# Seven products for eight from the third batch on in a kernel of attention and a two-layer product, with the second weight prepared during the first two batches

## The chip, the cores and the metric

The kernel runs on one core of one Trainium2 chip. A time is the device time in microseconds (us) of one execution, and of several executions the median is given. A profiled execution also has a span, from the first to the last instruction that the profiler recorded, which is a little shorter than its device time. The engines are named as the profile names them: PE (TensorE) multiplies, with PEld for its weight loads; DVE (VectorE) and ACT (ScalarE) work on tiles; POOL (GpSimd) works on tiles and starts the loads; SP (SyncE) starts the transposing copies and the stores.

## The reference

Eight sequences ("batches") of 384 tokens pass through an attention with 16 query heads and 4 key/value heads of 64 columns, and the result through two matrix products with a squared relu between them.

```python
q: (8, 16, 384, 64)   k, v: (8, 4, 384, 64)
w_in: (1024, 2048)    w_out: (2048, 1024)

scores = np.matmul(q, k.transpose(0, 1, 3, 2)) / np.sqrt(64)
attn = softmax(scores)
x = np.matmul(attn, v).transpose(0, 2, 1, 3).reshape(8 * 384, 16 * 64)
h = np.maximum(x @ w_in, 0.0)
return (h * h @ w_out).astype(np.float32)
```

## The kernel before

**Stages.** Each batch b has an up product (384 rows of x by w_in, "up-b") and a down product (384 rows of the squares by w_out, "down-b"), one after the other. Between their matmuls lie the attention pieces of the next batches: the scores q·k (L437; their exponentials go to `expT`, L447), the probabilities by the values (L463 on all 128 rows of the array, L504 on two concurrent halves of 64 rows), the division by the row sums (L472 and L478), and the largest magnitude of each piece of x (L1438).

**Order.** The program is not written in the order in which it runs. A class `Recorder` takes every instruction group with what it reads and writes and an assumed cost, and keeps a clock for each engine. A loop picks TensorE's next piece among the candidates by these clocks, and between the pieces `upkeep` hands out work to the other engines from queues, each entry with a condition: `d_q` (sums for the down product), `w_q` (parts of w_in), `w2_q` (parts of w_out), `lazy` and `m_q` (ranges of x). Then each engine gets its list in that order, with semaphore waits where the readers and writers demand them. An engine works its list strictly in order.

**Seven products for eight.** From batch `SB` = 2 on, the up product splits both factors into two by two blocks and makes seven block products where the plain way makes eight (`strassen`, L884), with sums of blocks of x (L642) and of w_in (L724, L729; w_in itself is scaled in place by L738, with one subtraction, L742). The block products are evicted from the accumulator banks by L855, L860, L863 and L868, and then squared (L770, L778, L782). From batch `FAST` = 3 on, the down product does the same with pairs of row tiles (`pair_of`). A batch has three row tiles of 128. Pair "A" joins tiles 0 and 1 of batch b. Every second batch also makes pair "D" of the tile 2 of the batch before and its own. The copy L1157 keeps that earlier tile. `sum_ops` makes the sums of a pair (L1138, part of them on GpSimd), `done` the evictions (L1054 to L1062) and one addition on GpSimd (L1091). Since batches 3 to 7 are five, tile 2 of batch 7 is left without a partner. It is multiplied the plain way (`downs`, `down_part`, L1249), after L1162 has restored a block of w_out.

The matmuls of seven products run as two concurrent streams on the halves of the array (L924 for the down product). The plain down products of batches 0 and 1, and the plain tile of batch 7, use all 128 rows (L1249). The plain down product of batch 2 goes through the stream too. The up product of batch 0 uses whole rows (L563), that of batch 1 halves (L600, `quad`, evicted by L613, squared by L618). Plain results are evicted by `store` (L1274, L1281).

**Preparation of w_out.** The block sums are kept in f16, so w_out is first scaled to a common range. `fold2` takes sixteen sums of squares (L1174, on ScalarE), `roots2` turns them into bounds by two shifts (L1180, L1181), `top_of` takes the largest (L657) and spreads it (L659), `top_spread` sends it through TensorE (L669) and back (L673), and `o_units` makes the factor (L1186, L1188). Then `scaled2` writes scaled blocks into `area` (L1191), `less2` subtracts them from each other (L1199), `here2` scales w_out in place (L1191) once nothing plain reads it any more, and `apart2` makes the last difference (L1206). In the kernel before, the conditions of `w2_q` place the folds between 101.2 and 120 us, the maximum at the end of down-1, the blocks from there to 167.7 us, their differences in down-2, the scaling in place between 173.2 and 190 us, and the last difference behind it in up-3.

**Space.** `expT` of a batch has two halves, the second of them in `area`, where the blocks of w_out and two of the eight `hr` tiles live later too. `LEAN` = 3 is the first batch that has only the first half, so that at most half of its scores can be made before its values are multiplied. `LATE` = 4 is the first batch whose values are loaded straight to their place.

The two conditions that place the maximum and the scaled blocks of w_out:

```python
w2_q.append((lambda: not spread_q and not w_q, [], roots2, "vector"))
def cleared():
    return "o_beta" in R.writer and x_done[LEAN - 1] == NKC and up_over()
```

## Time and profile before

| | us |
|---|---|
| three runs | 404.82, 405.20, 405.56 |
| median | 405.2 |
| profiled execution, its device time | 404.96 |
| its span | 403.1 |

Stages by the first and last matmul of each, in us of the span:

| batch | up | down | what of w_out is prepared there |
|---|---|---|---|
| 0 | 15.8 to 52.1 | 52.1 to 73.1 | |
| 1 | 73.2 to 103.3 | 103.3 to 126 | folds, maximum, first block |
| 2 | 126 to 151 | 151 to 176 | blocks, differences, first of the scaling in place |
| 3 | 176 to 203.4 | 203.4 to 219.5 (A) | rest of the scaling in place, last difference |
| 4 | 219.5 to 244 | 244 to 272 (A, D) | |
| 5 | 272 to 297.5 | 297.5 to 311.1 (A) | |
| 6 | 311.1 to 336.3 | 336.3 to 361 (A, D) | |
| 7 | 361 to 380.5 | 380.5 to 403.1 (A, one plain tile) | |

How to read the profile's lines: a row of a timeline begins with the start, then the length, the engine, the line of the kernel and the operation, then what it writes and reads, with partitions by elements. A row of the waits gives the waiting engine and line, the engine and line that ended the wait, and the total, the number and the mean. A row of the stages gives a stretch, its length, and the busy time of each engine with the number of its instructions.

### The profile page before, as it was taken

Reading aid. Unit: us, or ns where it says so; the run is one execution under the profiler, and the core shown is the slowest. Engines: PE = TensorE matmul, PEld = TensorE weight load, DVE = VectorE, ACT = ScalarE, POOL = GpSimd, SP = SyncE. Lnnn points to the kernel's source line nnn. Section 1 sums busy time; section 2 is a strip of 40 time slices with the busy share of each in tenths; the row PEclk is TensorE's granted clock in tenths of the full one; section 3 lists DMA queues with packets and bytes.
Section 4 is the critical chain, followed back from the end, with each engine's and each line's share of the span. In section 5 each row is a group of like instructions: output and inputs, shape, how many; then the busy total and the mean of one; then the engine's idle time right before and its main releaser. Section 6 shows DMA issues by size and latency. Waiting matters only on the chain. (4 is left out here: it accounts for less than half of the span.)

```text
span 403.1 us, 15107 instructions
## 1 busy us (share of the span) xinstructions
PE 392.0 (97%) x6784; PEld 292.4 (73%) x6784; DVE 313.2 (78%) x646; ACT 261.5 (65%) x365; POOL 145.5 (36%) x167
## 2 busy tenths in 40 slices
PE   8999999999998999998998999999999999999997
PEld 5665754456546998788874998749996998649944
DVE  3699879924967879998989797867878888936655
ACT  7949940087985998897884677735985686115610
POOL 8675600168230230044563444223532152114500
PEclk9999999999999999999999999999999999999999
DMA  9999999993993172699677632598160311212003
GB/s 173 191 197 185 208 187 186 146 246 56 156 147 123 32 93 42 137 157 113 78 105 121 115 43 57 114 179 161 23 101 29 101 33 33 80 52 81 4 28 130
DMA packets 97200, 44.75 MB, mean 111 GB/s; under 512 B 77552, under 2 KB 91120, under 8 KB 97136
## 3 DMA queue, kind: packets, MB, share of 16 engines
q0 software_dynamic: 36672, 17.44, 34.7%
q1 hardware_dynamic: 59792, 25.86, 30.8%
q8 instruction: 53, 0.87, 0.9%
q10 hardware_dynamic: 672, 0.49, 0.4%
q14 instruction: 11, 0.09, 0.1%
HBM read 35.65 MB, written 12.58 MB: 120 GB/s over the span
## 5 line engine op out<-in xcount | busy, mean ns | idle before, releaser
L447 ACT ACTIVATE expT<-ps 128x1024 bf16<-128x1024 f32 (+1 forms) x118 | 115.3, 1012 | 19.7 <-PE ps L437 19.2
L884 PE MATMUL ps<-xT,w_in_sb 64*128 64x192 f16 x1152 | 85.5, 243 | 0.9 <-DVE y_sb L1062 0.6
L924 PE MATMUL ps<-w_out_sb,h2T 64*128 64x512 f16 (+1 forms) x464 | 84.9, 376 | 0.0
L884 PEld LDWEIGHTS ps<-xT,w_in_sb 64*128 64x128 f16 x1152 | 70.7, 94 | 4.9 <-DVE y_sb L1062 1.0
L782 POOL TENSOR_TENSOR h2T<-hr 128x384 f16<-128x384 f32 (+1 forms) x49 | 40.5, 843 | 49.0 <-ACT hr L770 48.6
L437 PE MATMUL ps<-qT,kT 64*128 64x256 bf16 (+2 forms) x336 | 52.1, 324 | 0.5 <-DVE qT L408 0.2
L884 PE MATMUL ps<-s_all,wx 64*128 64x192 f16 x768 | 52.2, 242 | 0.0
L1249 PE MATMUL ps<-w_out_sb,h2T 128*128 128x512 bf16 (+3 forms) x240 | 49.4, 365 | 0.0
L868 DVE TENSOR_TENSOR hr<-ps,hr 128x384 f32<-128x384 f32 x72 | 39.7, 555 | 10.3 <-PE ps L884 6.9
L924 PEld LDWEIGHTS ps<-w_out_sb,h2T 64*128 64x128 f16 (+1 forms) x464 | 38.9, 94 | 11.0 <-DVE hr L855 0.4
L924 PE MATMUL ps<-area,xT 64*128 64x512 f16 x224 | 43.6, 376 | 1.0 <-DVE y_sb L1056 1.0
L884 PEld LDWEIGHTS ps<-s_all,wx 64*128 64x128 f16 x768 | 44.0, 94 | 0.8
L600 PE MATMUL ps<-xT,w_in_sb 64*128 64x384 bf16 x448 | 42.7, 323 | 0.5 <-DMA xT<-area 0.3
L770 ACT ACTIVATE hr<-hr,bits 128x384 f32<-128x384 f32 x59 | 35.0, 608 | 10.1 <-DVE hr L868 9.8
L1249 PEld LDWEIGHTS ps<-w_out_sb,h2T 128*128 128x128 bf16 (+1 forms) x240 | 22.4, 98 | 24.9 <-issue 0.6
L504 PE MATMUL ps<-v_aug,expT 64*128 64x65 bf16 x1440 | 38.2, 190 | 1.6 <-issue 1.3
L504 PEld LDWEIGHTS ps<-v_aug,expT 64*128 64x128 bf16 x1440 | 35.2, 94 | 3.2 <-issue 1.7
L884 PE MATMUL ps<-xT,wx 64*128 64x192 f16 x384 | 33.2, 243 | 0.0
L860 ACT COPY hr<-ps 128x384 f32<-128x384 f32 x29 | 13.8, 477 | 29.9 <-PE ps L884 29.0
L884 PE MATMUL ps<-s_all,w_in_sb 64*128 64x192 f16 x384 | 33.0, 242 | 0.0
L600 PEld LDWEIGHTS ps<-xT,w_in_sb 64*128 64x128 bf16 x448 | 21.4, 94 | 15.9 <-DMA xT<-area 0.6
L863 DVE COPY hr<-ps 128x384 f32<-128x384 f32 x43 | 23.7, 555 | 8.1 <-PE ps L884 6.1
(147 smaller groups left out, 744.7 us busy)
## 6 DMA issues: line engine op xcount, KB each, us to landing
out_dram<-y_sb SPq DMA_DIRECT2D x44, 256.0 KB, 2.4
w_in_sb<-in_moe_w_in_dram POOLq DMA_DIRECT2D x8, 512.0 KB, 14.6
w_out_sb<-in_moe_w_out_dram POOLq DMA_DIRECT2D x4, 1024.0 KB, 28.4
q_st<-in_q_dram POOLq DMA_DIRECT2D x19, 192.0 KB, 4.7
q_st<-in_q_dram POOLq DMA_DIRECT2D x4, 384.0 KB, 23.6
k_st<-in_k_dram POOLq DMA_DIRECT2D x6, 192.0 KB, 5.1
wx<-in_q_dram POOLq DMA_DIRECT2D x2, 384.0 KB, 7.7
out_dram<-area SPq DMA_DIRECT2D x3, 256.0 KB, 4.6
```

What stands on the lines that cost most here:

```text
L437: mm = pe.matmul(ps[:, base + x, m * wide:(m + 1) * wide], kT[at(b)][64 * x:64 * x + 64, u, :], q_cols(b, u // NJ, x, c0, c0 + wide))
L447: R.add("scalar", lambda e: e.activation(dst, src, AF.Exp, scale=0.125), reads=keys, writes=[("expT", slot(b, u), t) for u, _, _ in pieces ...
L504: m = pe.matmul(ps[:, p[x], n * DP:n * DP + D + 1], w, v_aug[b % 2][r, g * NJ + j, 0:D + 1], start=(n + j + y == 0), stop=(n + j + y == 2 ...
L600: m = pe.matmul(bank(4 + xs[x])[:, 0:S], w_in_sb[r, kc, c * 128:(c + 1) * 128], xT[b % NXT][r, kc, :], start=(phase < 2 and kc == 0), stop ...
L770: R.add("scalar", lambda e, val=val, to=to: e.activation(val, val, AF.Relu, scale=to), reads=[("hr", r)] + by, writes=[("hr", r)], cost=0. ...
L782: n = R.add(eng, lambda e, dst=dst, two=two: e.tensor_tensor(dst, two, two, ALU.mult), reads=[("hr", r)], writes=keys, cost=0.77 if other ...
L860: R.add("scalar", lambda e: e.copy(hr[r][:, :], src), reads=[("bank", at)], writes=[("hr", r)], cost=0.45, after=hr_read.pop(r, ()))
L863: R.add("vector", lambda e: e.tensor_copy(hr[r][:, :], src), reads=[("bank", at)], writes=[("hr", r)], cost=0.48, after=hr_read.pop(r, ()))
L868: R.add("vector", lambda e: e.tensor_tensor(hr[r][:, :], src, hr[r][:, :], ALU.add), reads=[("bank", at), ("hr", r)], writes=[("hr", r)], ...
L884: return lambda pe: pe.matmul(bank(at)[:, f * h:f * h + h], w[r, kc, c:c + 128], m[r, kc, :], start=(prod in (1, 5, 2) and y + f + kc == 0 ...
L924: return lambda pe: pe.matmul(bank(p.at)[:, 0:512], p.a(k, r), p.w(k, r), start=start, stop=stop, skip_group_check=True)
L1249: m = pe.matmul(bank(i)[:, 0:n], h2[:, c, i3 * 128:(i3 + 1) * 128], w2[:, c, c0:c1], start=(c == 0), stop=(c == NFC - 1))
```

## The change

Three of the constants that place things are lowered by one: `FAST` 3 to 2, `LEAN` 3 to 2, `LATE` 4 to 3. Batches 2 to 7 make their down products by pairs, which leaves no tile without a partner, so the plain tile of batch 7 and L1162's restoring of w_out are gone. With an even number of batches the D pairs fall to batches 3, 5 and 7.

- In the last batch the D pair ends in the order 7, 4, 3, and its last product is made on whole rows in two pieces of 384 and 128 columns (`whole_product`, new). `added`, `put` and `send` take a range of columns for it, and the second piece's store has a semaphore of its own.
- The folds of w_out go to a place of their own (`o_top`, in `s_all`), and may start once the folds of w_in are done, which is during down-0. The maximum may follow while w_in's parts are still waiting, in up-1. The blocks may be written as soon as batch 1's x is complete.
- `less2` and `apart2` may go to VectorE or GpSimd, whichever clock is free; GpSimd's assumed cost is 2.3 us.
- Half of w_in's scaling in place may begin in the last tiles of up-1, and on ScalarE.
- Score bursts of batches 2 and 3 may be placed inside down-1 (`loose`).
- Batch 1's and later evictions rotate over six `hr` tiles instead of eight. The largest magnitudes of x are taken for batch 2 too.

```diff
-    SB, LEAN, LATE, FAST = 2, 3, 4, 3
-    TINY, DOWN = 2.0 ** -100, 2.0 ** -12
+    SB, LEAN, LATE, FAST = 2, 2, 3, 2
+    TINY, DOWN, TAIL = 2.0 ** -100, 2.0 ** -12, 384
...
+    o_top = s_all.ap().rearrange("p a n c -> p (a n c)")[:, 2048:2080].bitcast(f32)
...
-                r = hr_n[0] % NHR
+                r = hr_n[0] % (NHR - 2 * (b > 0))
...
-                    r = hr_n[0] % NHR
+                    r = hr_n[0] % (NHR - 2 * (b > 0))
...
-              reads=["w_u1"], writes=[("w_16", q)], cost=3.6 if eng == "scalar" else 1.2, after=free)
+              reads=["w_u1"], writes=[("w_16", q)], cost=3.6 if eng == "scalar" else 1.75, after=free)
...
-        first, second, rest, carry = stream(products(b))
+        prods = products(b)
+        final = prods.pop() if b == B - 1 else None
+        first, second, rest, carry = stream(prods)
...
-            rest += [zipped([], carry[0] + carry[1])] + downs(b)
+            rest += [zipped([], carry[0] + carry[1][:1]), zipped([], carry[1][1:])] + whole_product(final)
...
+    def whole_product(p):
+
+        def part(c0, c1, at, fresh):
+            def mm(pe):
+                for k in range(p.n):
+                    m = pe.matmul(bank(at)[:, c0:c1], p.a(k, slice(0, 128)), p.w(k, slice(0, 128))[:, c0:c1], start=fresh and k == 0, stop=k == p.n - 1,
+                                  skip_group_check=True)
+                return m
+
+            def piece():
+                R.add("tensor", mm, reads=need, writes=[("bank", at)], cost=p.n * ((c1 - c0) / 2400 + 0.004))
+                p.done(at, c0, c1)
+
+            need = [r for k in range(p.n) for r in p.need(k)]
+            return NKC, need, [at], piece
+
+        return [part(0, TAIL, p.at, False), part(TAIL, 512, order[0], True)]
+
...
-            out += [first(4, b1)] + [second(*x) for x in ((1, b2), (2, b3), (5, b1), (6, b2), (7, b3), (3, b1), (4, bz))]
+            ends = ((7, b3), (3, b1), (4, bz)) if b < B - 1 else ((7, b3), (4, bz), (3, b1))
+            out += [first(4, b1)] + [second(*x) for x in ((1, b2), (2, b3), (5, b1), (6, b2)) + ends]
...
-        out[-1].done = lambda at: (tail_open.discard(b), last(at))
+        out[-1].done = lambda *at: (tail_open.discard(b), last(*at))
...
-        def added(at, g, a, to):
+        def added(at, g, a, to, c0=0, c1=512, after=()):
...
-            R.add("vector", lambda e: e.scalar_tensor_tensor(y_sb[z], bank(at), gs[g], y_sb[y], ALU.mult, ALU.add),
-                  reads=[("bank", at), ("g", g), ("y", y)], writes=[("y", z)], cost=0.68)
-
-        def put(who, x, name):
+            R.add("vector", lambda e: e.scalar_tensor_tensor(y_sb[z][:, c0:c1], bank(at)[:, c0:c1], gs[g], y_sb[y][:, c0:c1], ALU.mult, ALU.add),
+                  reads=[("bank", at), ("g", g), ("y", y)], writes=[("y", z)], cost=0.68 if c1 - c0 > 128 else 0.27, after=after)
+
+        def put(who, x, name, c0=0, c1=512):
...
-            send(bb, i3, 512 * x, 512 * x + 512, ys[name])
-
-        def done(prod, at):
+            send(bb, i3, 512 * x + c0, 512 * x + c1, ys[name], c0)
+
+        def done(prod, at, *cols):
...
+                ys["bank"] = at
...
+                if b == B - 1 and pair == "D":
+                    added(ys["bank"], g1, "b2", "b2", TAIL, 512, (R.writer[("y", ys["p5"])],))
...
-                added(at, g1, "b2", "b2")
-                put(one, 1, "b2")
+                added(at, g1, "b2", "b2", *cols)
+                put(one, 1, "b2", *cols)
...
-            return Product(at, a, w, lambda k: na(k) + nw(k), lambda at: done(prod, at), prod not in (3, 6))
+            return Product(at, a, w, lambda k: na(k) + nw(k), lambda *at: done(prod, *at), prod not in (3, 6))
...
-        R.add("scalar", lambda e: e.activation(junk, w2_piece(q, z, w_out_sb), AF.Square, accum_out=w_top[:, n:n + 1]),
-              reads=[("w_out",) + QS[q], "junk2"], writes=[("w_top", n), "junk2", ("hr", 6), ("hr", 7)], cost=1.15)
+        R.add("scalar", lambda e: e.activation(junk, w2_piece(q, z, w_out_sb), AF.Square, accum_out=o_top[:, n:n + 1]),
+              reads=[("w_out",) + QS[q], "junk2"], writes=[("o_top", n), "junk2", ("hr", 6), ("hr", 7)], cost=1.15)
...
-        t = w_top.bitcast(mybir.dt.int32)
-        keys = [("w_top", n) for n in range(16)]
+        t = o_top.bitcast(mybir.dt.int32)
+        keys = [("o_top", n) for n in range(16)] + [("S", 2)]
...
-        top_of(w_top, *keys)
+        top_of(o_top, *keys)
...
-    def less2(n, m, z):
+    def less2(n, m, z, eng="vector"):
...
-        R.add("vector", lambda e: e.tensor_tensor(a, a, c, ALU.subtract),
-              reads=[("T2", n, z), ("T2", m, z)], writes=[("T2", n, z)], cost=0.62)
+        R.add(eng, lambda e: e.tensor_tensor(a, a, c, ALU.subtract),
+              reads=[("T2", n, z), ("T2", m, z)], writes=[("T2", n, z)], cost=0.62 if eng == "vector" else 2.3)
...
-    def apart2(z):
-        R.add("vector", lambda e: e.tensor_tensor(w2_piece(3, z), w2_piece(3, z), w2_piece(2, z), ALU.subtract),
-              reads=[("w2", 3, z), ("w2", 2, z)], writes=[("w2t", z)], cost=0.6)
+    def apart2(z, eng="vector"):
+        R.add(eng, lambda e: e.tensor_tensor(w2_piece(3, z), w2_piece(3, z), w2_piece(2, z), ALU.subtract),
+              reads=[("w2", 3, z), ("w2", 2, z)], writes=[("w2t", z)], cost=0.66 if eng == "vector" else 2.3)
...
-            for i3 in range(0 if b < SB else 2, NJ):
-                last = b == B - 1 and (jj, i3) == (1, NJ - 1)
-                for c0, c1 in ((512, 896), (896, 1024)) if last else ((512 * jj, 512 * jj + 512),):
+            for i3 in range(NJ if b < SB else 0):
+                for c0, c1 in ((512 * jj, 512 * jj + 512),):
...
+                flags.add(("plain", b, NJ * jj + i3))
...
-    def send(b, i3, c0, c1, yb):
-        ysl = y_sb[yb][:, 0:c1 - c0]
+    def send(b, i3, c0, c1, yb, y0=0):
+        ysl = y_sb[yb][:, y0:y0 + c1 - c0]
...
-                            reads=[("y", yb)], writes=[("out", b, i3, c0)], dma=f"y{yb}", cost=0.6)
+                            reads=[("y", yb)], writes=[("out", b, i3, c0)], dma=f"y{yb}" + "z" * (y0 > 0), cost=0.6)
...
-                                                  spread_q.append((b % 2, lambda: (v_unit(b), measured.add(b))))), lambda: b != LEAN or pairs >= 8 * b))
+                                                  spread_q.append((b % 2, lambda: (v_unit(b), measured.add(b))))), lambda: b != 3 or pairs >= 8 * b))
...
+    def in_place(qq):
+        act, dve = [max(R.clock[x], R.clock["tensor"]) for x in ("scalar", "vector")]
+        w_in_place(qq, "scalar" if qq < 3 and act + 3.6 <= dve + 1.75 + 0.0 else "vector")
+
+    def columns_over():
+        return up_over() or ff["b"] == 1 and len(ff["tiles"]) <= 4
+
...
-        w_q.append((up_over, [], lambda qq=qq: w_in_place(qq, "vector")))
+        w_q.append((columns_over if qq < 2 else up_over, [], lambda qq=qq: in_place(qq)))
...
-        return "o_beta" in R.writer and x_done[LEAN - 1] == NKC and up_over()
-
-    w2_q = [(lambda: "w_u0" in R.writer and (ff["b"] > 1 or ff["b"] == 1 and below()), [("w_out",) + QS[n // 4]], lambda n=n: fold2(n), "scalar") for n in range(16)]
-    w2_q.append((lambda: not spread_q and not w_q, [], roots2, "vector"))
+        return "o_beta" in R.writer and x_done[LEAN - 1] == NKC
+
+    w2_q = [(lambda: not any(len(x) > 3 for x in w_q), [("w_out",) + QS[n // 4]], lambda n=n: fold2(n), "scalar") for n in range(16)]
+    w2_q.append((lambda: "w_u0" in R.writer and not spread_q, [], roots2, "vector"))
...
-            w2_q.append((cleared, [], (lambda *eng, n=n, qq=qq, z=z: scaled2(n, qq, z, *eng)) if m is None else (lambda n=n, m=m, z=z: less2(n, m, z)), "any" if m is None else "vector"))
+            w2_q.append((cleared, [], (lambda *eng, n=n, qq=qq, z=z: scaled2(n, qq, z, *eng)) if m is None else (lambda *eng, n=n, m=m, z=z: less2(n, m, z, *eng)), "any" if m is None else "either"))
...
-        w2_q.append((lambda: True, [], lambda z=z: apart2(z), "vector"))
+        w2_q.append((lambda: True, [], lambda *eng, z=z: apart2(z, *eng), "either"))
...
-                load_v(n)
+                if n < LATE:
+                    load_v(n)
...
-            lead = {"scalar": 0.1, "vector": 0.5 if ff["b"] == FAST else -9 if m_q or lazy else 1.0 if below() else 0.1}
-            able = [x for x in ("vector", "scalar") if eng in (x, "any") and R.clock[x] <= now + lead[x]]
+            lead = {"scalar": 0.1, "vector": -9 if m_q or lazy else 0.6 if below() else 0.4}
+            lead["gpsimd"] = 0.0
+            able = [x for x in {"any": ("vector", "scalar"), "either": ("vector", "gpsimd")}.get(eng, (eng,)) if R.clock[x] <= now + lead[x]]
...
-            w2_q.pop(0)[2](*(able[:1] if eng == "any" else ()))
+            w2_q.pop(0)[2](*(able[:1] if eng in ("any", "either") else ()))
...
+            loose = SB <= b <= SB + 1 and not split and ff["b"] == SB - 1 and len(ff["tiles"]) < 4
...
-            if b and not split and not beside:
+            if loose and b > SB:
+                ok = ok and (R.clock["scalar"] <= now + -99 or not (w2_q and w2_q[0][0]()))
+            if b and not split and not beside and not loose:
...
-                if b and not split and not beside:
+                if b and not split and not beside and not loose:
...
-                cand.append((t, 4 if beside else 0, "sc"))
+                cand.append((t, 4 if beside or loose and b > SB else 0, "sc"))
...
-        if split and at_edge and len(ff["tiles"]) < 4 and not (sc_q and sc_q[0][1]):
+        if split and at_edge and len(ff["tiles"]) < 4 and (not (sc_q and sc_q[0][1]) or ff["b"] == SB - 1):
...
+            widest_of(b, c - 3) if b >= FAST else None
...
+            if b >= FAST:
+                wide_q.append((b, c))
+                if c == 7:
+                    m_q.append((b, lambda b=b: widest_of(b)))
...
-            if b and not split and not beside:
+            if b and not split and not beside and not loose:
...

```

## The prediction

> **What bounds the kernel now.** I read the page's first two parts, then the waits of TensorE over the whole span, then the busy times by stage, and only then single instructions. "Up-b" and "down-b" are the up and the down product of batch b (0 to 7).
>
> ```profile
> span 403.1 us, 15107 instructions
> PE 392.0 (97%) x6784; PEld 292.4 (73%) x6784; DVE 313.2 (78%) x646; ACT 261.5 (65%) x365; POOL 145.5 (36%) x167
> ...
> PE ps L669 <- DVE top_w L659: 2.2, 2, 1.1
> PE ps L504 <- issue: 1.3, 1, 1.3
> PE ps L924 <- DVE y_sb L1056: 1.0, 1, 1.0
> ...
> PE ps L884 <- DVE y_sb L1062: 0.6, 2, 0.3
> ```
>
> TensorE is the bound: it is busy for 392.0 of 403.1 us, and its waits are few and can be listed one by one. So fewer matmul columns shorten the span one for one, and every other engine counts only where it makes TensorE wait. The stages show where that happens now:
>
> ```profile
> core 0: us, PE busy (x) PEld busy (x) DVE busy (x) ACT busy (x) POOL busy (x), PEclk, DMA share, GB/s
> 52.10:73.10 21.00, 21.00 (x104) 9.32 (x100) 16.93 (x32) 2.79 (x5) 1.69 (x1) 1.00 1.18 169
> ...
> 103.30:126.00 22.70, 21.57 (x107) 9.41 (x104) 17.91 (x34) 16.81 (x31) 5.17 (x5) 1.00 0.94 155
> ...
> 176.00:203.40 27.40, 25.74 (x740) 23.93 (x736) 24.67 (x54) 22.82 (x35) 14.64 (x16) 1.00 0.87 117
> 203.40:219.50 16.10, 14.04 (x146) 8.73 (x142) 14.74 (x27) 11.30 (x14) 7.27 (x8) 1.00 0.78 103
> 219.50:244.00 24.50, 24.01 (x668) 22.60 (x670) 20.37 (x49) 15.39 (x24) 11.67 (x14) 1.00 0.41 77
> ```
>
> The first column is the stretch, then its length, then the busy time of each engine. Down-0 (first row) is full. Down-1 (second) lacks 1.13 us of TensorE work: that is the wait for the maximum of w_out (L669 behind L659). Up-3, down-3 and up-4 (the last three) lack 1.66, 2.06 and 0.49 us, together 4.2 us. In up-3 the last parts of w_out are still being made, down-3 is the first stage with pairs, and VectorE is busy for 24.67 of 27.40 and 14.74 of 16.10 us in these two. In batch 5, where nothing is prepared, the same stages lack nothing. The granted clock is 1.00 throughout.
>
> **The change, part by part.** (1) *Fewer matmuls.* A plain down product takes 96 matmuls of 128 rows by 512 columns for three row tiles; a pair by seven products takes 56 where the plain way takes 64. Before, batches 3 to 7 make 7 pairs and one plain tile (7 x 56 + 32 = 424), and batch 2 is plain (96): 520. After, batches 2 to 7 make 9 pairs and nothing plain: 504. Two concurrent halves of such a matmul start 0.216 us after the two before them (five steps from 214.97 to 216.05 in TensorE's timeline of down-3). 16 x 0.216 = **-3.5 us**. The count is in the changed kernel's instruction order, so that the change does not do what it says is excluded.
>
> (2) *Switches between whole rows and halves.* L437 (scores) works on 64-row halves, L1249 and L463 on all 128 rows. Before, the scores of batch 2 all lie in up-1, whose L600 also works on halves. With LEAN = 2 only half of expT may be filled ahead, so nine of its eighteen score bursts, and five of batch 3, move into down-1, between L1249 and L463. Changes between 128 and 64 rows in TensorE's order rise from 48 to 70. The price of one:
>
> ```profile
> 16.18 0.39 PE L437 MATMUL ps<-qT,kT 64*128 64x512 bf16 x2
> 16.50 0.51 PE L538 MATMUL ps<-ident,o_sb 128*128 128x128 bf16 x6
> ...
> 181.19 0.38 PE L437 MATMUL ps<-qT,kT 64*128 64x512 bf16 x2
> 181.41 0.82 PE L884 MATMUL ps<-s_all,wx 64*128 64x192 f16 x16
> ```
>
> The first number of a row is its start. The same burst takes 0.32 us to the next start before 128-row work and 0.22 us before halves: 0.10 us for leaving, and entering costs as much (16.18 lies 0.42 us after the start of two L563 at 15.76, which need 2 x 0.16). 22 x 0.10 = **+2.2 us**; bounds 1.5 and 3.
>
> (3) *Start of up-1.* The maximum of w_out is now finished there: two shifts, L657 and L659 stand on VectorE ahead of the first L613, and L669 stands on TensorE between the pieces of the first quad. VectorE is late here already (the last L729 ends at 78.2 us and the second quad waits until 79.2 for banks 4 and 5). The four take 0.16 + 0.18 + 0.17 + 0.23 = 0.74 us; with the hand-over to TensorE **+0.9 us**; bounds 0 and 1.5 (the three L673, L1186, L1188 behind it also late). The sixteen squares of w_out move under down-0, where ScalarE works 2.79 of 21.0 us: 16 x 1.06 = 17 us fit, so they cost nothing; without that cover up-1's exponentials would start late.
>
> (4) *Down-1, the crowded stage.* By the changed order VectorE does there: 8 L472 and L478 (0.19 + 0.56, 6.0), two L738 (2.7), L742 (2.3), three L1199 (2.0), six L1274 (4.1), eight L1438 (4.3), four L642 (2.2), two L1191 (1.0) and eight small ones (1.7): 26.3 us. TensorE has 20.9 (the 96 matmuls of down-0) + 4.5 (144 L463 at 98.8 to 103.3, half of them just ahead of the stage) + 14 bursts x 0.22 + 2.2 of switches = 30.7 us. That leaves 4.4 us of slack, if nothing blocks VectorE. But GpSimd now makes 8 of the 12 L1199 subtractions, 6 of them here, and three of the four L1206 later. No row has one on GpSimd; the nearest has half the elements:
>
> ```profile
> L1138 POOL TENSOR_TENSOR xT<-h2T 128x512 f16<-128x512 f16 x5 | 5.8, 1159 | 11.7 <-PE ps L884 11.7
> ...
> 207.18 2.14 DVE L1138 TENSOR_TENSOR xT<-xT,h2T 128x512 f16<-128x512 f16 x1
> ...
> 207.12 1.90 POOL L1157 COPY area<-h2T 128x2048 f16<-128x2048 f16 x1
> ```
>
> So one costs 2 x 1.16 = 2.3 us, 13.9 for six. The last two rows show VectorE and GpSimd excluding each other: an L1138 that usually takes 0.42 us took 2.14 because a copy on GpSimd had started 0.06 us before, and the 1.0 us wait on L1056 above is what followed from it. L738, L742, L1199, L642 and L1191 (10.2 us) are of the kind that can be caught so; L478, L1274 and L1438 read PSUM or one tensor and run beside GpSimd. In the changed order L738, L1199, L738 and L742 stand against four subtractions in a row on GpSimd. If each waits 2.3 us less one 0.69 us copy that fits beside it, VectorE needs 26.3 + 4 x 1.6 = 32.7 us, 2.0 over TensorE; behind them are queued the evictions and the L1274 copies that free banks 6 and 7, and L1249 waits for those. With 0.3 us for the first burst, which waits for two evictions, **+2.3 us**. Bounds: 0 (VectorE first each time) and 9.5 (all six whole).
>
> (5) The wait for L659 near the end of down-1 goes: **-1.1 us**; another L669 takes its place for batch 2's range, inside the count of (4).
>
> (6) *Batches 2 to 4.* The 4.2 us of up-3, down-3 and up-4 go from there, since w_out is ready earlier and the first pairs lie in down-2. Part returns one batch earlier: eight scalings by L1191 (0.48 us on VectorE) and some of the L1206 lie in up-2, and down-2 has the same sums and copy on GpSimd as down-3 had. But its copy of the first product stands on ScalarE in the changed order, not behind the blocked sum, and L659 comes before the last three products, not after them. The 1.3 us without a releaser have no known cause and are left to chance. I take 1.2 us as returning: **-3.0 us**; bounds -4.2 and +1.
>
> (7) The last stage: one more pair in place of a plain tile, its last product in two pieces (384 and 128 columns) as the last plain one was. The 128-column eviction (0.35 us) may stand behind the 384-column one by 0.2 us: counted as nothing, bounds -0.5 and +0.5.
>
> Sum: 403.1 - 3.5 + 2.2 + 0.9 + 2.3 - 1.1 - 3.0 = 400.9 us of span. The profiled execution took 404.96 us, 1.86 more than its span, and the median of the three runs (405.2) lies 0.24 above it: **403.0 us**.
>
> **The rivals.** *The exclusion decides* (slower). All six blocks in down-1 cost 1.6 us: 26.3 + 9.6 - 30.7 + 0.3 = 5.5 in place of 2.3, and the three L1206 on GpSimd give up half of (6): +3.2 + 1.5, so 405.6 of span and 407.7 us. It decides from 8 us of blocks in down-1 on (6.4 are in the forecast): with 1.5 us of (6) gone, that passes 406.0 us. For it: the 2.14 us row and 10.2 us of catchable work. Against: of the ten VectorE instructions that this trace shows stretched by over 0.1 us beside GpSimd, TensorE waited behind four at most. The Trainium skill, page "SBUF — State Buffer", section "Who interferes with whom", says that a VectorE instruction with two SBUF inputs, or in a two-port mode, and a GpSimd instruction exclude each other for the whole of the one that came first. The 2.14 us row agrees; by that rule this rival is the likelier the more subtractions begin just ahead of VectorE's.
>
> *The stalls only move*: (6) is nought because up-2 and down-2 lose what up-3 and down-3 lost. 403.9 of span, 406.0 us. For it: the same rows of work on the same engines. Against: the order of L659 and of the first copy.
>
> *Everything fits*: (4) is nought and all 4.2 us of (6) are kept: 400.9 - 2.3 - 1.2 = 397.4, so 399.5 us. For it: 4.4 us of slack; against: the lateness of VectorE at the start of up-1.
>
> **How the numbers follow.** About 0.2% (0.8 us) is what a measurement of this kernel can tell from no change: faster is below 404.4, slower above 406.0. The forecast has 0.50 (its own range 400.8 to 405.2; 0.42 of it faster, 0.06 same, 0.02 slower), the exclusion 0.20 (0.19 slower, 0.01 same), moved stalls 0.17 (0.02 faster, 0.08 same, 0.07 slower), everything fits 0.13 (faster). Faster 0.57, same 0.15, slower 0.28. The range, 399.3 to 407.6, leaves out the half of the exclusion's chance above it and the better end of the last rival.
>
> **What would show it.** (1) 992 matmuls of the stream on halves, 16 at a new line, 192 of the plain kind. (2) Gaps of 0.1 us around each L437 in down-1. (3) L669 waiting some 0.9 us near 79 us. (4) In down-1, two-input VectorE instructions of 2 us beside L1199 on GpSimd, and L1249 waiting on L1274. (5) and (6) the stages of batch 3 without idle TensorE. I am wrong if down-1 loses over 5 us beside its switches, or if batches 2 and 3 together lose more than batches 3 and 4 did.

## The result, and the profile after

The changed kernel takes 418.0 us, median of four runs (416.9 to 418.3), against 405.4 us in the same series: ratio 1.0303, 95% interval 1.0272 to 1.0334. It is slower, and beyond the range. Every series of runs has its own runs of the kernel before (medians 405.0 to 405.5 us), and each ratio is to those; the changed kernel was timed in the first series alone, so differences to its 418.0 us reach across series. Two executions far above the others of their kernel, 573.2 us in subs_and_slot and 809.5 us in and_squares, are left out of the ratios and of what follows. The first parts of its page, and its waits of TensorE over the whole span (total, number, longest):

```profile
span 415.1 us, 15143 instructions
...
PE 393.8 (95%) x6764; PEld 286.8 (69%) x6770; DVE 333.2 (80%) x658; ACT 271.1 (65%) x372; POOL 174.8 (42%) x182
...
PE   8999999995999998998999999899999999999995
...
PEclk9999999999899999999999999999999999999999
```

```profile
PE ps L670 <- DVE top_w L660: 3.8, 3, 3.2
PE ps L885 <- issue: 1.8, 2, 1.0
PE ps L927 <- DVE y_sb L1084: 1.6, 3, 0.6
PE ps L601 <- DVE hr L614: 1.4, 1, 1.4
PE ps L927 <- DVE xT L1163: 1.4, 1, 1.4
```

The span is 12.0 us longer. TensorE is busy for about as long as before (393.8 us for 392.0), but idle for 21 us where it was idle for 11. The tenth slice, 93 to 104 us, is half empty, and the clock, full throughout before, dips just behind it. One wait of 3.2 us stands out. The line numbers of the changed kernel are higher: L660, L670 and L674 are the old L659, L669 and L673; L614, L619 and L625 the eviction and the squares of up-1; L739 the scaling of w_in (old L738); L1452 the range of a batch's values; L1163, L1182 and L1116 the sum, the copy and the addition of the pairs; L1216, L1224 and L1231 the scaling and the two subtractions.

The stages of up-1 to up-3, and down-4 (stretch, its length, busy time of PE, PEld, DVE, ACT, POOL, granted clock):

```profile
73.70:107.30 33.60, 27.80 (x359) 16.93 (x360) 32.98 (x57) 15.49 (x18) 18.85 (x18) 0.95 0.84 142
107.30:136.60 29.30, 28.77 (x202) 12.16 (x205) 24.49 (x39) 24.30 (x24) 17.50 (x11) 1.00 0.70 114
136.60:165.10 28.50, 26.36 (x704) 24.01 (x702) 26.31 (x59) 22.87 (x32) 16.50 (x16) 1.00 0.52 69
165.10:180.60 15.50, 15.24 (x215) 8.36 (x211) 14.88 (x29) 11.66 (x14) 8.26 (x7) 1.00 0.56 96
180.60:209.70 29.10, 26.42 (x768) 25.25 (x767) 23.86 (x51) 19.26 (x30) 16.02 (x18) 1.00 0.87 114
...
261.60:276.70 15.10, 13.60 (x138) 8.22 (x134) 12.97 (x27) 11.68 (x15) 4.88 (x6) 1.00 0.67 82
```

Batch 1 (the first two rows) takes 62.9 us where it took 52.9: this is 10.0 of the 12.0 us. Up-1 has 5.8 us of idle TensorE (before 0.5) and a clock of 0.95, though nine score bursts have left it. From up-2 to the last matmul the kernel needs 274.1 us, before 274.5: TensorE is busy for 3.9 us less there, but idle for 3.4 us more. The span ends 4.4 us behind the start of the last matmul, before 2.6, and 0.6 us is lost ahead of batch 1.

What happens in up-1 is read from three timelines, of VectorE, GpSimd and TensorE (start, length):

```profile
89.24 4.25 DVE L739 TENSOR_SCALAR w_in_sb<-w_in_sb,bits 128x4096 f16<-128x4096 bf16 x2
...
95.27 4.74 DVE L625 TENSOR_TENSOR h2T<-hr 128x384 bf16<-128x384 f32 x1
...
100.40 1.00 DVE L1452 TENSOR_REDUCE bits<-v_aug 128x1 f32<-128x384 bf16 x2
101.43 0.15 DVE L658 TENSOR_REDUCE bits<-bits 128x1 f32<-128x2 f32 x1
101.62 0.74 DVE L660 CAST top_w<-bits 128x128 bf16<-128x128 f32 x1
```

```profile
93.82 2.14 POOL L1224 TENSOR_TENSOR area<-area 128x1024 f16<-128x1024 f16 x1
95.91 1.61 POOL L619 TENSOR_TENSOR h2T<-hr 128x384 bf16<-128x384 f32 x2
97.47 2.11 POOL L1224 TENSOR_TENSOR area<-area 128x1024 f16<-128x1024 f16 x1
```

```profile
94.47 3.42 PE L601 MATMUL ps<-xT,w_in_sb 64*128 64x384 bf16 x40 [1.41 <-DVE hr L614]
...
97.73 1.46 PE L601 MATMUL ps<-xT,w_in_sb 64*128 64x384 bf16 x16
...
102.42 0.20 PE L670 MATMUL ps<-ident,top_w 64*128 64x64 bf16 x2 [3.22 <-DVE top_w L660]
```

A square on VectorE that takes 0.55 us elsewhere takes 4.74. It starts while a subtraction runs on GpSimd, and GpSimd goes on without a gap to two squares and a second subtraction. VectorE comes through only when that row of four is over, at 99.58. Behind the square stand the range of batch 3's values and its spreading (L1452, L658, L660), and L670, in order on TensorE, waits for it. An earlier wait, of 1.41 us, follows two scalings of w_in (L739) that take 4.25 us where one takes 1.28 alone. Behind the long wait the clock falls, as the same stretch shows, cut where the clock changes (column before the last two):

```profile
100.31:103.72 3.41, 1.30 (x27) 0.86 (x27) 3.34 (x8) 0.25 (x1) 0.82 (x1) 1.00 0.02 5
103.72:107.14 3.42, 3.28 (x62) 3.12 (x60) 3.32 (x10) 3.42 (x5) 2.60 (x4) 0.50 0.00 0
107.14:110.55 3.41, 3.36 (x18) 1.16 (x16) 2.94 (x6) 2.03 (x2) 3.41 (x2) 1.00 0.30 58
```

TensorE works at half speed for 3.4 us. That makes it busy for some 1.7 us longer, an estimate from half of 3.4 us; how much of it the kernel loses in the end is a question for the runs.

### The profile page after: what moved, and what is told of

Its sections match the earlier page's. It is cut to its first block, busy times and chain, and to the rows that moved or that the text cites. A ratio compares the mean times of both kernels' runs of the same rounds, so it can differ in the third digit from the quotient of the medians.

```text
span 415.1 us, 15143 instructions
## 1 busy us (share of the span) xinstructions
PE 393.8 (95%) x6764; PEld 286.8 (69%) x6770; DVE 333.2 (80%) x658; ACT 271.1 (65%) x372; POOL 174.8 (42%) x182
## 4 chain that ended last, share of the span: by engine, by line
PE 65%; DVE 16%; issue 8%; POOL 5%; DMA 3%; ACT 2%; POOLq 0%; DVEq 0%
PE ps L885 25%; PE ps L927 18%; PE ps L438 6%; PE ps L1273 5%; PE ps L505 4%; PE ps L601 4%; POOL area L1224 2%; DVE y_sb L1084 2%; PE ps L464 2%; DMA xT<-o_sb 2%; DVE hr L614 2%; DVE h2T L625 2%; DVE xT L1163 2%; DMA q_st<-in_q_dram 1%; PE ps L564 1%
## 5 line engine op out<-in xcount | busy, mean ns | idle before, releaser
L448 ACT ACTIVATE expT<-ps 128x1024 bf16<-128x1024 f32 (+1 forms) x127 | 124.7, 1015 | 28.5 <-PE ps L438 28.3
L927 PE MATMUL ps<-w_out_sb,h2T 64*128 64x512 f16 x336 | 73.3, 376 | 1.0 <-DVE y_sb L1084 0.6
L783 POOL TENSOR_TENSOR h2T<-hr 128x384 f16<-128x384 f32 x53 | 42.8, 826 | 58.3 <-ACT hr L771 58.1
L927 PE MATMUL ps<-area,xT 64*128 64x512 f16 x288 | 56.0, 376 | 1.4 <-DVE xT L1163 1.4
L1273 PE MATMUL ps<-w_out_sb,h2T 128*128 128x512 bf16 x186 | 43.2, 380 | 0.3
L1116 POOL TENSOR_TENSOR y_sb<-y_sb 128x512 f32<-128x512 f32 x9 | 12.1, 1345 | 62.6 <-DVE y_sb L1084 62.6
L1084 DVE SCALAR_TENSOR_TENSOR y_sb<-ps,bits,y_sb 128x512 f32<-128x512 f32 (+2 forms) x38 | 26.9, 722 | 14.0 <-PE ps L927 6.3
L1077 ACT ACTIVATE y_sb<-ps,bits 128x512 f32<-128x512 f32 x18 | 12.3, 687 | 39.1 <-PE ps L927 36.3
L927 PEld LDWEIGHTS ps<-w_out_sb,h2T 64*128 64x128 f16 x336 | 29.3, 94 | 11.3 <-DVE y_sb L1084 2.2
L927 PE MATMUL ps<-area,h2T 64*128 64x512 f16 x144 | 36.1, 376 | 0.0
```

The lines of the kernel that those rows point to most:

```text
L448: R.add("scalar", lambda e: e.activation(dst, src, AF.Exp, scale=0.125), reads=keys, writes=[("expT", slot(b, u), t) for u, _, _ in pieces ...
L783: n = R.add(eng, lambda e, dst=dst, two=two: e.tensor_tensor(dst, two, two, ALU.mult), reads=[("hr", r)], writes=keys, cost=0.77 if other ...
L927: return lambda pe: pe.matmul(bank(p.at)[:, 0:512], p.a(k, r), p.w(k, r), start=start, stop=stop, skip_group_check=True)
L1084: R.add("vector", lambda e: e.scalar_tensor_tensor(y_sb[z][:, c0:c1], bank(at)[:, c0:c1], gs[g], y_sb[y][:, c0:c1], ALU.mult, ALU.add), re ...
L1273: m = pe.matmul(bank(i)[:, 0:n], h2[:, c, i3 * 128:(i3 + 1) * 128], w2[:, c, c0:c1], start=(c == 0), stop=(c == NFC - 1))
```

## The experiments

Theory A: GpSimd's new subtractions hold VectorE out, for a whole row of instructions if need be. Theory B: VectorE simply has too much to do in batch 1. In the surgical experiments the planner is left as it was and only the engine of some instructions is changed afterwards (`plan=` names the engine whose clock the planner advances), so that the order on every engine stays the same apart from them.

**The subtractions on VectorE.**

```diff
-        R.add(eng, lambda e: e.tensor_tensor(a, a, c, ALU.subtract),
+        R.add("vector", lambda e: e.tensor_tensor(a, a, c, ALU.subtract), plan=eng,
...
-        R.add(eng, lambda e: e.tensor_tensor(w2_piece(3, z), w2_piece(3, z), w2_piece(2, z), ALU.subtract),
+        R.add("vector", lambda e: e.tensor_tensor(w2_piece(3, z), w2_piece(3, z), w2_piece(2, z), ALU.subtract), plan=eng,
```

> The changed kernel with its eleven subtractions on GpSimd (eight of blocks of w_out into area, three of the last difference) issued on VectorE at the same places; every other instruction keeps its engine and order. Theory A (GpSimd holds VectorE out, and a row of GpSimd instructions back to back holds it out for the whole row): the square of 4.74 us at 95.27 falls to 0.55, the wait of 3.2 us for the maximum at 102.4 and the granted clock of 0.50 behind it go; 418.0 - 3.5 - 1.7 - about 1 in up-2 = 411 to 413 us, with VectorE's stretched time down from 23 to under 12 us although it has 11 x 0.69 = 7.6 us more work. Theory B (VectorE simply has too much to do in up-1 and down-1): more work on it makes it worse, 419 to 424 us.

Measured: 411.3 us, ratio 1.0164 (1.0132 to 1.0195), 6.7 us less than the changed kernel. Two rows of VectorE in up-1, where the long square stood (its L626 is the square, its L661 the spreading):

```profile
96.87 1.01 DVE L626 TENSOR_TENSOR h2T<-hr 128x384 bf16<-128x384 f32 x2
...
99.50 0.67 DVE L661 CAST top_w<-bits 128x128 bf16<-128x128 f32 x1
```

The square and the one behind it together take 1.01 us, no wait on the maximum of over 0.2 us is left in batch 1, and the clock is 1.00 in all three stages of batch 1 and up-2. VectorE does 7.6 us more work and the kernel is faster: theory B falls, theory A stands.

**Only the two subtractions of up-1.** The same edit, for the first two subtractions that the planner gives to GpSimd.

> The changed kernel with only the two subtractions that GpSimd makes in up-1 issued on VectorE; the other nine stay on GpSimd, all order stays. Theory A with its place in up-1: nearly the whole gain of subs_on_vector comes from these two, 412 to 413 us, clock 1.00 through up-1 and down-1, and the long exclusions in down-1 (2.5 and 3.1 us) stay and cost little, since TensorE has other work there. If the exclusions of down-1 and up-2 count as much as those of up-1: 414.5 to 416.

Measured: 412.5 us, ratio 1.0161 (1.0131 to 1.0192). By the medians these two carry 5.5 of the 6.7 us; by the ratios, each to its own series, all of it. Batch 1 takes 58.9 us in this trace, for 62.9. In down-1 of this kernel a scaling by L740 still takes 3.14 us beside GpSimd, and TensorE has no wait of over 0.4 us there: the place was up-1, not down-1.

**The squares on ScalarE.**

```diff
-                        hr_read[r] = (R.add("vector", lambda e, c=c, r=r: e.tensor_tensor(
-                            h2T[:, c, :], hr[r][:, :], hr[r][:, :], ALU.mult),
+                        hr_read[r] = (R.add("scalar", lambda e, c=c, r=r: e.activation(
+                            h2T[:, c, :], hr[r][:, :], AF.Square), plan="vector",
```

> The changed kernel with the six squares of up-1 that stand on VectorE issued on ScalarE, which is idle for 10.9 us there; the subtractions stay on GpSimd and all other order stays. Theory A in the form that a two-input VectorE instruction is caught by the row of GpSimd instructions: with none at 95.27 the maximum comes on time, 418.0 - 3.5 - 1.7 = 412.5 to 413.5 us. If instead the block only moves on to the next VectorE instruction that can be caught (the copy of the maximum, the subtraction behind it), the gain is 1 to 2 us: 416 to 417. Theory B: six squares less are 3.3 us less work in a crowded stage, 415 us, with the long wait shorter but there.

Measured: 414.9 us, ratio 1.0238 (1.0210 to 1.0267), between the two forms of theory A and at the figure that theory B had named. VectorE and GpSimd:

```profile
98.29 3.94 DVE L661 CAST top_w<-bits 128x128 bf16<-128x128 f32 x1
```

```profile
95.62 2.14 POOL L1225 TENSOR_TENSOR area<-area 128x1024 f16<-128x1024 f16 x1
97.71 1.61 POOL L620 TENSOR_TENSOR h2T<-hr 128x384 bf16<-128x384 f32 x2
99.28 2.11 POOL L1225 TENSOR_TENSOR area<-area 128x1024 f16<-128x1024 f16 x1
101.34 0.81 POOL L335 COPY v_aug<-k_st 128x768 bf16<-128x768 bf16 x1
```

With no square in the way the next instruction is caught: the spreading copy, 0.22 us by itself, takes 3.94, through two squares, a subtraction and a copy. TensorE waits 1.3 us for it instead of 3.2, and the clock does not fall. So the time alone would have fitted theory B, but B has no reason for a copy of 3.94 us, nor for the gain above with more work on VectorE: the block is GpSimd's row, whichever of these instructions stands on VectorE.

**GpSimd's copy in four, in the kernel before.** This asks whether VectorE gets in between two GpSimd instructions.

```diff
-                "gpsimd", lambda e: e.tensor_copy(h2x[:, :, :], h2_16[:, :, 256:384]), reads=keys,
-                writes=[("h2x", b), ("h2x", b - 2)] + X_OVER, cost=2.0), True))
+                "gpsimd", lambda e, n=n: e.tensor_copy(h2x[:, 4 * n:4 * n + 4, :], h2_16[:, 4 * n:4 * n + 4, 256:384]), reads=keys,
+                writes=[("h2x", b), ("h2x", b - 2)] + X_OVER, cost=0.5) for n in range(4)], True))
```

> The kernel before with the copy of tile 2 on GpSimd cut into four of a quarter each, back to back. Theory A in its strong form (VectorE stays out for a whole row of GpSimd instructions): the sum in down-3 still takes some 2.1 us, and the time stays at 405.0. If VectorE gets in between two GpSimd instructions: the sum takes 0.9 us or less, the wait of 1.0 us goes, 404.0 us.

Measured: 406.4 us, ratio 1.0016 (0.9999 to 1.0033). The two places where it runs, down-3 and down-5:

```profile
206.87 2.27 POOL L1157 COPY area<-h2T 128x512 f16<-128x512 f16 x4
206.92 2.50 DVE L1138 TENSOR_TENSOR xT<-xT,h2T 128x512 f16<-128x512 f16 x1
...
301.42 2.72 POOL L1157 COPY area<-h2T 128x512 f16<-128x512 f16 x4 [3.55 <-ACT h2T L778]
...
302.91 0.75 DVE L1138 TENSOR_TENSOR xT<-xT,h2T 128x512 f16<-128x512 f16 x1
```

In down-3 the sum loses to all four pieces. In down-5 it comes in after one, and the next piece is stretched. The strong form holds in one place and not in the other. In up-2 of the changed kernel, too, VectorE came in after one (L660, 0.98 us, at 159.23). What decides it is open.

**The clock, in the kernel before.** Two reductions of 1.2 us are put on VectorE ahead of the maximum of w_out.

```diff
+        for n in range(2):
+            R.add("vector", lambda e, n=n: e.tensor_reduce(bits[:, 58 + n:59 + n], w2_piece(0, 0, w_out_sb), mybir.AxisListType.XY, ALU.max),
+                  reads=[("w_out", 0, 0)], writes=[("spare", n)], cost=0.0)
         top_of(w_top, *keys)
```

> The kernel before with two reductions of 1.2 us each put on VectorE ahead of the maximum of w_out at the end of down-1, at no change of any order; TensorE's wait there grows from 1.3 to about 3.7 us. Theory C (after a wait of TensorE of over 3 us the granted clock falls to 0.5 for some 3.4 us): 405.4 + 2.4 + 1.7 = 409.5 us, with granted clocks near 0.5 in the 3 us behind the wait. Rival (the clock fell in the changed kernel for another reason): 407.8 us and a clock of 1.00 throughout.

Measured: 408.4 us, ratio 1.0095 (1.0064 to 1.0126). The profiled execution, cut in the same way, and a place of a kernel that comes further down, planned_on_vector:

```profile
122.44:125.85 3.41, 1.39 (x7) 0.42 (x5) 3.34 (x8) 0.00 (x0) 0.00 (x0) 1.00 0.60 225
125.85:129.27 3.42, 1.70 (x6) 0.69 (x7) 3.23 (x9) 0.01 (x1) 0.00 (x0) 0.50 0.09 32
129.27:132.68 3.41, 3.41 (x15) 1.52 (x14) 1.57 (x3) 1.90 (x2) 0.00 (x0) 0.50 0.12 44
...
192.87:196.28 3.41, 1.52 (x45) 1.21 (x41) 1.47 (x4) 2.34 (x4) 2.42 (x3) 1.00 1.49 124
196.28:199.70 3.42, 3.42 (x60) 3.26 (x56) 1.43 (x3) 1.59 (x3) 0.00 (x0) 0.50 1.09 83
```

TensorE waits for 3.75 us, the clock falls to 0.50 after 2.0 of them and stays there for 6.8 us. It is not the same each time: the four executions had mean clocks of 0.992, 1.000, 0.996 and 0.996, and spans of 408.6, 406.3, 406.6 and 406.6 us. So a wait of this length can bring one stretch of slow clock, two or none. One stretch made 0.3 us here and two 2.3, a rough price from so few executions. In the changed kernel all four executions had a mean of 0.994 to 0.996. The rows, and those of the changed kernel above, show more: the clock keeps to stretches of 3.41 us, and each stretch at 0.50 follows one in which TensorE was busy for 1.70 us or less. In planned_on_vector a wait of 1.9 us was enough for that.

**A store tile of its own at the end.**

```diff
+                if b == B - 1 and pair == "D":
+                    slot("a4")
+                else:
+                    ys["a4"] = ys["a3"]
-                added(at, g2, "a3", "a3")
-                put(two, 0, "a3")
+                added(at, g2, "a3", "a4")
+                put(two, 0, "a4")
```

> The changed kernel with the sum of the last stage's product 4 written to a store tile of its own, so that it need not wait for the addition on GpSimd that reads the tile. Theory: the three last evictions begin at 409.2 and not at 410.79, and the end follows the last matmul by 2.6 us as before the change, not by 4.4: 416.4 to 416.8 us. Rival (the last evictions wait for the stores to free their tiles): 418 us.

Measured: 415.3 us, ratio 1.0255 (1.0233 to 1.0277). The end follows the start of the last matmul by 3.5 us instead of 4.4, so 1.0 us of the 2.7 is shown; the rest is open. The clock does not account for it: the two executions with a mean clock of 0.996 took 415.4 and 415.7 us, the two at 1.000 took 415.0 and 415.2, so by these four one stretch of slow clock is worth some 0.4 us, not 1.7. Together with the first edit:

> The changed kernel with both mends that were run alone, the subtractions on VectorE and the store tile of its own in the last stage, at the same order otherwise. If the two are independent, as theory A and the tail's theory have it (one in batch 1, one behind the last matmul), their gains add: 418.0 - 6.7 - 2.7 = 408.6 us, 409.3 if the tail is worth only the 2.0 us that the two traces show. If they share a cause, 411 us.

Measured: 411.8 us, ratio 1.0166 (1.0148 to 1.0184): no gain over subs_on_vector is to be seen, whose own runs lie between 410.7 and 413.1. Why the 1.0 us of the tile is not seen is open; the next kernel, which has the tile too, does end 3.5 us behind its last matmul. One more GpSimd instruction taken off up-1:

```diff
-        R.add(eng, lambda e: e.copy(dst, src) if eng == "scalar" else e.tensor_copy(dst, src),
+        plan, eng = eng, "scalar" if b == 3 and R.clock["tensor"] < 200 else eng
+        R.add(eng, lambda e: e.copy(dst, src) if eng == "scalar" else e.tensor_copy(dst, src), plan=plan,
```

> As subs_and_slot, with one more GpSimd instruction of up-1, the copy of 2.45 us that doubles batch 3's keys, issued on ScalarE. Theory A: the two scalings in place that take 1.84 and 2.48 us beside it fall to 1.28 each, and the wait of 1.65 us at 95.1 falls under 0.5: about 1.3 us less than subs_and_slot, 407.3 to 408. Theory B (VectorE is late there by its own work, six scalings and eight evictions before it): the wait keeps over 1 us, gain under 0.5.

Measured: 409.9 us, ratio 1.0115 (1.0097 to 1.0134): 1.9 us less than subs_and_slot, though over the range, which had counted on a full gain from the tile. The wait at 95, by the profile 1.41 us, has become 0.17. The two scalings fall to 3.04 us together, not quite to 2 x 1.28. Theory A again.

**Planned anew.** Here GpSimd is no longer offered to the planner (`"either"` becomes `"vector"`), and in the second kernel `columns_over` becomes `up_over` as well.

> The changed kernel in which the planner itself may put the subtractions on VectorE alone (GpSimd no longer offered), with the store tile of its own; the whole order is planned anew. Theory A: no row of subtractions on GpSimd, so no wait of over 2 us in up-1 and a clock of 1.00: within 1.5 us of subs_and_slot, 407.5 to 410.5. Theory B: the planner's clocks now show VectorE as full, so batch 1 would lose as much as in the changed kernel: 414 or more.

> As planned_on_vector, with the part of the change undone that lets w_in's scaling in place begin in up-1; it stands in down-1 again, as before the change. If the crowded start of up-1 is the rest of the loss (its idle time is 3.3 us over that of the kernel before when the subtractions are on VectorE), up-1 gains 1.5 to 2 us and down-1 loses less than 1: 407 to 408.5. If down-1 is as full as up-1, it only moves: 409 to 411.

Measured: 420.2 us, ratio 1.0377 (1.0350 to 1.0405), and 422.8 us, 1.0437 (1.0396 to 1.0479): both missed. Batch 1 of the first is in fact 7.4 us shorter than in the changed kernel (55.5 us), but its down-2 takes 27.4 us, of which TensorE is busy for 20.9, at a clock of 0.88. The largest wait of that stage:

```profile
PE ps L438 <- ACT expT L448: 4.1, 6, 1.6
```

The parts of w_out come later (the last of its scalings in place at 173.2 us, where it was 146.0), and down-2 waits for them (1.2 us) and for ScalarE; that this is because the planner now hands VectorE the subtractions only where its clock is free is not shown. These two tell about the planner and not about the parts they were to undo.

**GpSimd relieved further from batch 2 on**, first with the copy of tile 2 (L1182) on ScalarE and the additions (L1116) on VectorE, on top of and_copy_on_scalar and in the kernel before:

```diff
-                "gpsimd", lambda e: e.tensor_copy(h2x[:, :, :], h2_16[:, :, 256:384]), reads=keys,
+                "scalar", lambda e: e.copy(h2x[:, :, :], h2_16[:, :, 256:384]), plan="gpsimd", reads=keys,
...
-                R.add("gpsimd", lambda e: e.tensor_tensor(y_sb[z], y_sb[z], y_sb[y], ALU.add),
+                R.add("vector", lambda e: e.tensor_tensor(y_sb[z], y_sb[z], y_sb[y], ALU.add), plan="gpsimd",
```

> As and_copy_on_scalar, and GpSimd loses two more kinds of work from batch 2 on: the copy of a batch's tile 2 goes to ScalarE, the addition of product 7 to VectorE, at the same places in the order. Theory A: the waits of 1.6 us in down-4 and 0.9 in down-6 behind a blocked sum, and those of some 0.9 behind blocked sums of x, go: 409.9 - 1.4 - 0.6 - 0.9 = 406.5 to 407.5 us. If ScalarE's two-microsecond copy stands ahead of evictions that TensorE waits for, 409 to 411.

> The kernel before with the same two moves, the copy of tile 2 to ScalarE and the additions of product 7 to VectorE. Theory A: the wait of 1.0 us in down-3 behind the sum of 2.14 us goes, with some tenths elsewhere: 405.0 - 1.0 - 0.5 = 403.5 us. Rival as above: 405 to 406.

Measured: 407.8 us, ratio 1.0054 (1.0035 to 1.0072), just over the forecast, and 406.4 us, 1.0025 (1.0000 to 1.0051), no gain. In both the copy on ScalarE now stands ahead of exponentials that scores wait for (2.1 and 1.3 us in all). Then the copy on VectorE instead, with the last stage's addition left on GpSimd; in the second kernel also the last five squares of up-1 on ScalarE; in the third only the copy, in the kernel before:

> As gpsimd_relieved, but the copy of tile 2 stands on VectorE instead of ScalarE, and the last stage's addition stays on GpSimd. Theory A: a copy on VectorE costs VectorE some 0.8 us where the exclusion cost it 1.5 to 2.3, and ScalarE's exponentials are free again: the waits of 1.4 us in down-2 and 0.9 in down-4 go, and 0.5 us of the tail: 407.8 - 2.3 = 405.0 to 406.0 us. If VectorE is full in down-2, TensorE waits for it instead: 407 to 408.5.

> As relieved_on_vector, with the last five squares of up-1 on ScalarE (idle there for 6.3 us) instead of GpSimd. Theory A: the square of 1.56 us and the subtraction of 1.33 us on VectorE fall to 0.55 and 0.68, and some of the waits of 0.6 and 1.0 us at 98.8 and 101.2 with them: 0.5 to 1.2 us less than relieved_on_vector. If those waits come from VectorE's own queue, no gain.

> The kernel before with only the copy of tile 2 moved from GpSimd to VectorE. Theory A: the sum of 2.14 us in down-3 falls to 0.42 at the price of a copy of about 0.8 us: the wait of 1.0 us in down-3 shrinks to under 0.4, 404.4 to 405.0 us. If VectorE's queue there is the bound, 405.4 or more.

Measured: 405.2 us, ratio 0.9995 (0.9981 to 1.0009); 404.4 us, 0.9982 (0.9967 to 0.9997); and 404.0 us, 0.9973 (0.9956 to 0.9990). The third at the place of the 2.14 us row that the prediction showed:

```profile
206.30 0.43 DVE L1139 TENSOR_TENSOR xT<-h2T 128x512 f16<-128x512 f16 x1 [1.01 <-ACT h2T L779]
206.76 0.42 DVE L1139 TENSOR_TENSOR xT<-xT,h2T 128x512 f16<-128x512 f16 x1
```

The sum takes 0.42 us, and down-3 1.2 us less. This smallest edit, on the kernel before, is 0.3% faster than it, a little better than forecast, with an interval that leaves out 1. With all edits together the changed order comes down by 13.6 us, to 0.2% under the kernel before, and does not pass the old order with its one copy moved: its 16 matmuls less are given back elsewhere, as the next section counts.

## Why the prediction was wrong

(1) *Fewer matmuls* holds: 16 of them are gone, and from up-2 on TensorE is busy for 3.9 us less. That it brings only 0.4 us from there to the last matmul is the idle time, counted under (6).

(2) *Switches* holds. Behind 52 us there are 32 changes between whole rows and halves, where there were 10. In down-1:

```profile
134.11 1.04 PE L1273 MATMUL ps<-w_out_sb,h2T 128*128 128x512 bf16 x4
135.08 0.39 PE L438 MATMUL ps<-qT,kT 64*128 64x512 bf16 x2
135.40 1.04 PE L1273 MATMUL ps<-w_out_sb,h2T 128*128 128x512 bf16 x4
```

Four L1273 are 4 x 0.216 = 0.86 us, and the burst starts 0.97 us behind them; the burst is 0.22 us, and the next L1273 starts 0.32 us behind it. So entering and leaving cost 0.10 us each. Taken so over all changes it is 3.2 us, before 1.0: the 2.2 of the forecast.

(3) *Start of up-1* holds: L670 waits 0.3 us at 79.6, and the wait for the transposed x ahead of it is 0.6 us where it was 0.3.

(4) *Down-1, the crowded stage* is the step that failed. It named the mechanism and put it into the wrong stage. It counted that six of the eight subtractions stand in down-1 and priced those, at one instruction's length each, and left the two in up-1 without a price, where squares on both engines and the range of batch 3 stand around them. In down-1 VectorE is stretched much as foreseen (L1224 2.52 us at 112.24, L739 3.14 us at 114.68), but TensorE is idle there for 0.5 us in all, where (4) took 2.3. In up-1 it is idle for 5.8 us, where (3) took 0.9: one block lasted as long as a row of four and cost 3.2 us, and behind it the clock fell. The scalings of w_in that the change had moved into up-1, which no term prices either, cost 1.4 us; that wait went only when the copy of the keys left GpSimd. The run with only the two subtractions moved is 5.5 us faster. Neither the row nor the clock was in the bounds. The rival "the exclusion decides" had the right cause with the wrong place, and its price of 407.7 us was 10 us short. The Trainium skill, page "SBUF — State Buffer", section "Who interferes with whom", was right on who blocks whom; that the one blocked may lose to several instructions in a row is what these runs add.

(5) holds: the wait near 124 us is gone, and the new L670 at 129.24 waits for 0.3 us.

(6) *Batches 2 to 4* failed in sign. Instead of 4.2 us shrinking to 1.2 they grew to 7.1: 2.1 us in up-2, 2.7 in up-3, 1.5 in down-4 and 0.8 elsewhere. In up-2 a spreading copy of 0.98 us stands behind L1231 on GpSimd. In up-3 1.8 us have no releaser. In down-4 a sum of 2.71 us (L1163 at 266.20) begins while GpSimd issues a load and is over only behind the copy L1182, so the wait of the old down-3 has only moved, as "the stalls only move" had it; and with the copy on VectorE that wait is gone. Batches 2 and 3 together lose 5.6 us, more than the 4.2 that batches 3 and 4 had lost: one of the signs of being wrong that the prediction had named.

(7) *The last stage* was counted as nothing and costs 1.8 us.

```profile
409.41 1.27 POOL L1116 TENSOR_TENSOR y_sb<-y_sb 128x512 f32<-128x512 f32 x1 [10.82 <-DVE y_sb L1084]
...
410.79 1.73 DVE L1084 SCALAR_TENSOR_TENSOR y_sb<-ps,bits,y_sb 128x512 f32<-128x512 f32 x3 [1.45 <-POOL y_sb L1116]
```

The sum of product 4 writes in place over a tile that the addition on GpSimd still reads, and the two last evictions are queued behind it. With a tile of its own the end comes 1.0 us sooner. Of the other 0.9, 0.3 lie on VectorE, where the eviction of 128 columns stands behind that of 384; most of the rest is that the stores of both pieces start only behind the last eviction (411.28 and 411.65 in own_slot), where before the first was under way by then (400.50 and 401.13).

In spans, 415.1 us stand against the 400.9 forecast. Of these 14.2 us up-1 has 5 to 6 (5.4 more of idle time and up to 1.7 of slow clock, less the 0.9 forecast), (6) has 5.9 and (7) has 1.8.

Leaving the subtractions off GpSimd would not have saved the forecast of 403.0: subs_on_vector measures 411.3. The changed order comes near it only in and_squares (404.4), where GpSimd is also relieved of work that it had before the change.

## What to carry to other kernels

Work moved to GpSimd may run not beside VectorE but in turn with it: bound its price by the longest row of GpSimd instructions without a gap, at every place where one lands, and ask what in-order work stands behind the VectorE instruction that will be caught. A wait of TensorE of about 2 us or more can bring a stretch of half clock behind it; in the few executions here one stretch made 0.3 to 0.4 us and two 2.3. And a change in the kind of tile (whole rows to halves) inside a stage is a term of its own: here it took 2.2 of the 3.5 us that the saved matmuls gave.

## What the runs showed of the hardware

VectorE lost to up to four GpSimd instructions in a row: 4.74 us for a square of 0.55, 3.94 for a copy of 0.22, 2.50 for a sum of 0.42; in other places it came in after one. One-input VectorE work is caught too, the scaling L739 (3.14 us for 1.28) and the spreading copy.

After a wait of TensorE of 3.2 to 3.75 us the granted clock was 0.50 for 3.4 or 6.8 us, or not at all, in executions of the same kernel. The Trainium skill, page "TensorE: Matmul & The Clock Gate", section "Part 1: The HAM clock gate", says that activity is watched in free-running windows of about 3.4 us and that an idle one brings half the clock. The lengths agree: every stretch between two changes of the clock in these traces is a whole number of 3.413 us. But a window need not be idle throughout: within the kernels the fall followed windows with 0.41 to 1.69 us of TensorE work, and windows with 1.81 us or more kept the full clock. One with 1.57 us, at the end of subs_on_vector, kept it too, so the border is not sharp here. Where the wait falls in its windows would explain why it differs from run to run.

Waits of TensorE without a releaser came and went in the same instruction stream: in up-3 they are 0.2 to 1.3 us in all in the five traces with the old order, and 1.6 to 2.2 us in nine traces that keep the changed order. Their cause was not tried.
